# Ranks of kept tokens as sums on TensorE, their comparisons on two engines, and a gate with fewer steps

## The chip, the cores and the metric

One core of one Trainium2 chip. The metric is the device time of one execution in microseconds, as the median of several runs. In the text TensorE is also PE (PEld are its weight loads), VectorE DVE, ScalarE ACT, GpSimd POOL, SyncE SP, as the profile has them.

## The reference

An attention of the delta rule (4 batches, 8 heads, 768 steps, heads of 48) feeds a mixture of experts with a capacity.

```python
for t in range(S):
    y[:, :, t] = einsum('bhd,bhde->bhe', q[:, :, t], state)
    v_old = einsum('bhde,bhd->bhe', state, kt)
    state = state + bt * einsum('bhd,bhe->bhde', kt, vt - v_old)
x = y.transpose(0, 2, 1, 3).reshape(3072, 384)
logits = x @ w_gate                      # 8 experts
expert_idx = argmax(logits, axis=1); gate_w = softmax(logits)[expert_idx]
for e in range(8):                       # at most 80 tokens an expert, the ones with the largest gate_w
    tok_idx = ...
    h = maximum(x[tok_idx] @ w1[e], 0); out[tok_idx] = gate_w[tok_idx] * (h @ w2[e])
```

The rows of tokens that are not kept are zero.

## The kernel before

**The attention loop.** Time is cut in 12 chunks of 64 steps. The loop `for j in range(NC)` (L1038) runs one step of the chain over the chunks and, ahead of it, prepares later chunks: `gram(j + 4)` makes the products of keys, `store` and `fetch` bring their 16x16 diagonal blocks through DRAM, `solve(j + 3)` (L404) inverts these on GpSimd with 14 pairs of small operations between a first product (L410) and a last copy (L418), `result_out` and `spread` bring the inverse back, and the `merge_` functions build the inverse of the whole chunk on TensorE. `scale_k` and `beta_mask` (L333, L338) are GpSimd's too. Chunk by chunk the chain makes R (L527), UB (L539), the new state and the outputs x.

**The order of work.** All of it is written out by hand: each engine executes its instructions in the order in which the program issues them. Work beside the loop is written as generators, which stand in a list `fillers`. `fill(us)` (L258) takes steps from the first one until the costs that they yield add up to `us`; a function that a generator yields waits in `due` until `point()` (L253) runs it. In a step j the calls come in this order: scale_k, beta_mask, chain_ks and `sums(j - 1)` (logits of the last chunk), point, merge_x4, a `fill(2.2)` for 6 <= j < 10, chain_tr, merge_y4, point, `fill(1.5)` (2.8 from j = 6 on), merge_p5, `solve(j + 3)`, chain, loads, outputs and the transposes `both(j + 4)`, `fill(6.6)` (8 from j = 6 on), point, merge_y5, out_t, `gram(j + 4)`, merge_p2, point.

**The gate.** A chunk gives two blocks of 128 tokens, so there are 24 blocks. `gate(m0, nm)` (L603) takes the logits of `nm` blocks and makes a one-hot of the argmax and the weight gw = 1 / sum of exp(logit - max). The exponential is a power of two (`two`, L639, made from the rounded quotient `n`) times a polynomial of the rest r, in Horner steps of one scalar_tensor_tensor each (L611). All of it is on VectorE, a step being 0.25 in the budget of `fill`, but for one call with `g=nc.gpsimd`. It is called for blocks 0 to 7 and 8 to 15 in `sort_group` (L688; appended to the fillers in the `sums` of j = 4 and j = 8), for blocks 16 to 19 on GpSimd at j = 10, and for blocks 20 to 23 after the loop (L1134). `gate_pool` (L673, GpSimd) packs the results for later products.

**The selection.** Blocks 0 to 15 are sorted by max8 operations; `choose_sorted` (L721) keeps at most 80 of them per expert ("old", their weights in AO). The 8 new blocks (16 to 23; `early` are the first four, `late` the others) are then compared with each other and with the old ones, and every token gets its rank:
- `beats` (L863) compares the weights of a group of new blocks, broadcast into GB1 (early) or GB2 (late), with those of block m, one weight per partition. It takes "less" for blocks ahead of m, "less or equal" for blocks behind it, and for m itself a tie mask with the triangle `tri`. The result H (4 buffers) is summed by `count` (L892) on TensorE with the one-hot of block m. For early against early all four calls are on GpSimd, at the end of j = 10 (L1099); the others follow the loop on VectorE.
- `against_old` (L847) compares the broadcast old weights ABC with new blocks (G), VectorE; the sums over G are TensorE's and ScalarE's.
- The rank among the old ones: 16 comparisons of 80x80 on GpSimd (L838, L839), a product with `trl` (L840), a sum (L841), and after the loop a reduction on VectorE (L842) into rankO.

After the loop the program issues: the counts of early against early, the sums over G, the weight loads 0 to 6 (`load_w`, SP queue), the transposes of `bcast_old` and `bcast_new(early)` with copies to ABC and GB1 by ScalarE, the late gate, its gate_pool, GB2, late against early, `against_old(late)`, the reduction into rankO, all against late, then slotO (L1148), one-hots and products that yield the row numbers idx_g.

**The experts.** Eight gathers on GpSimd (L1203) bring the rows; each expert is two groups of 96 pairs of products (L1237), with weights in 10 buffers.

Of the kernel before, what the change touches and what calls it, by code (L numbers as in the profile page):

```python
# [8 lines left out]
F32 = mybir.dt.float32  # L9
# [9 lines left out]
LN2_HI = 0.693145751953125  # L19
LN2_LO = 1.42860682030941723212e-6  # L20
ROUND = 12582912.0


@with_exitstack
def kernel(
# [22 lines left out]
    nc = tc.nc  # L48
# [100 lines left out]
    less = keep.tile([128, NN], F32, name="less")  # L149
    AO = keep.tile([cap, E], F32, name="AO")  # L150
    a5o = keep.tile([cap, E, 5], BF16, name="a5o")
    rankO = keep.tile([cap, E], F32, name="rankO")
    t1 = keep.tile([cap, E, cap], BF16, name="t1")
    tri = const.tile([128, 128], BF16, name="tri")
    nc.gpsimd.memset(tri, 1.0)
    nc.gpsimd.affine_select(out=tri, in_=tri, compare_op=Alu.is_gt, fill=0.0, base=0, pattern=[[1, 128]], channel_multiplier=-1)
    trl = const.tile([128, 128], BF16, name="trl")
    nc.gpsimd.memset(trl, 1.0)
    nc.gpsimd.affine_select(out=trl, in_=trl, compare_op=Alu.is_gt, fill=0.0, base=0, pattern=[[-1, 128]], channel_multiplier=1)
# [26 lines left out]
    with ExitStack() as actx:  # L186
# [71 lines left out]
        def fill(us, flush=False):  # L258

            while us > 0 and fillers:  # L260
                if due:
                    if not flush:
                        return
                    point()
                n = next(fillers[0], None)
                if n is None:
                    fillers.pop(0)
                elif callable(n):
                    due.append(n)
                else:  # L270
                    us -= n
# [331 lines left out]
        def gate(m0, nm, g=nc.vector):  # L603
# [5 lines left out]
            def stt(out, in0, scalar, in1, op0, op1):  # L609
                if g is nc.vector:  # L610
                    g.scalar_tensor_tensor(out=out, in0=in0, scalar=scalar, in1=in1, op0=op0, op1=op1)  # L611
# [27 lines left out]
            g.tensor_scalar(two, n, 127.0, 8388608.0, op0=Alu.add, op1=Alu.mult)  # L639
            yield 0.25  # L640
            r = tile_(full, F32, "r")
            stt(out=r, in0=n, scalar=-LN2_HI, in1=sc, op0=Alu.mult, op1=Alu.add)
            yield 0.25
# [6 lines left out]
            nc.vector.tensor_tensor(out=oh, in0=first, in1=fm.unsqueeze(2).to_broadcast(full), op=Alu.is_equal)  # L650
            yield 0.25
            ex = tile_(full, F32, "ex")
            g.tensor_scalar(ex, r, 1.0 / 5040.0, None, op0=Alu.mult)
            yield 0.25
            for f in (720.0, 120.0, 24.0, 6.0, 2.0, 1.0):
                stt(out=ex, in0=ex, scalar=1.0 / f, in1=r, op0=Alu.add, op1=Alu.mult)
                yield 0.25
            stt(out=ex, in0=ex, scalar=1.0, in1=two.bitcast(F32), op0=Alu.add, op1=Alu.mult)
            yield 0.25
            gw = gwN[:, m0 - NS : m0 - NS + nm] if new else tile_(full[:2], F32, "gw")  # L660
            sm = tile_(full[:2], F32, "sm")
# [11 lines left out]
        def gate_pool(m0, nm):  # L673
            full = [128, nm, E]
            oh, og = ohs[m0]
            rb = rhs[:, m0 : m0 + nm, :, :]
            nc.gpsimd.tensor_tensor(out=rb[:, :, :, 0], op=Alu.mult, in0=oh,
                                    in1=hi[:, m0 : m0 + nm].unsqueeze(2).to_broadcast(full))
            nc.gpsimd.tensor_scalar(rb[:, :, :, 1], oh, pp1[:, 0:1], None, op0=Alu.mult)
            rest = og  # L680
            for j in range(3):
                nc.gpsimd.tensor_copy(rb[:, :, :, 2 + j], rest)
                if j < 2:
                    nxt = gsm.tile([128, NT, E], F32, name=f"rest{j}")[:, :nm]
                    nc.gpsimd.tensor_tensor(out=nxt, in0=rest, in1=rb[:, :, :, 2 + j], op=Alu.subtract)
                    rest = nxt
# [34 lines left out]
        def choose_sorted(sl):  # L721
# [25 lines left out]
            W2 = [sl.tile([E, 2, 128], F32, name=f"W{i}") for i in range(2)]  # L747
# [87 lines left out]
            t2 = sl.tile([cap, E, cap], BF16, name="t2")  # L835
            for e in range(E):
                row, one_ = ABC[:cap, e], AO[:, e : e + 1]
                nc.gpsimd.tensor_scalar(t2[:, e], row, one_, None, op0=Alu.is_equal)  # L838
                nc.gpsimd.tensor_scalar(t1[:, e], row, one_, None, op0=Alu.is_gt)  # L839
            nc.gpsimd.tensor_tensor(out=t2, in0=t2, in1=trl[:cap, :cap].unsqueeze(1).to_broadcast([cap, E, cap]), op=Alu.mult)  # L840
            nc.gpsimd.tensor_tensor(out=t1, in0=t1, in1=t2, op=Alu.add)  # L841
            after.append(lambda: nc.vector.tensor_reduce(rankO, t1, axis=AX, op=Alu.add))  # L842
            yield from against_old(early, ABC, sl)

        counted, after = [], []

        def against_old(ms, ABC, sl):  # L847

# [11 lines left out]
                counted.append(sums_)  # L860
                yield 0.85

        def beats(eng, m, ms, GB, sl, own=True):  # L863

            L = len(ms)
            H = sl.tile([128, NN // 2 * 128], BF16, name="H", bufs=4)[:, : 128 * L]
            g = gwN[:, m : m + 1]
            a = sum(i < m for i in ms) * 128
            b = a + 128 * (m in ms)
            if a:  # L870
                eng.tensor_scalar(H[:, :a], GB[:, :a], g, None, op0=Alu.is_lt)
                yield 0.4
            if b < 128 * L:
                eng.tensor_scalar(H[:, b:], GB[:, b:], g, None, op0=Alu.is_le)
                yield 0.4
            if b > a:
                t = sl.tile([128, 128], BF16, name="tie", bufs=2)
                if eng is nc.vector:
                    eng.scalar_tensor_tensor(out=t, in0=GB[:, a:b], scalar=g, in1=tri, op0=Alu.is_equal, op1=Alu.mult)
                    yield 0.3  # L880
                    eng.scalar_tensor_tensor(out=H[:, a:b], in0=GB[:, a:b], scalar=g, in1=t, op0=Alu.is_lt, op1=Alu.add)
                    yield 0.3
                else:
                    eng.tensor_scalar(t, GB[:, a:b], g, None, op0=Alu.is_equal)
                    eng.tensor_scalar(H[:, a:b], GB[:, a:b], g, None, op0=Alu.is_lt)
                    eng.tensor_tensor(out=t, in0=t, in1=tri, op=Alu.mult)
                    eng.tensor_tensor(out=H[:, a:b], in0=H[:, a:b], in1=t, op=Alu.add)
            Hs[m, ms[0]] = H

        Hs = {}  # L890

        def count(m, ms):  # L892
            H = Hs.pop((m, ms[0]))
            for n, i in enumerate(ms):
                nc.tensor.matmul(S_ps[:, 0, 384 + E * i : 384 + E * i + E], lhsT=H[:, 128 * n : 128 * n + 128], rhs=ohN[:, m, :],
                                 start=False, stop=(m == NN - 1), skip_group_check=True)

        early, late = list(range(NN // 2)), list(range(NN // 2, NN))

# [27 lines left out]
        def drain(steps):  # L927
            for _ in steps:
                pass
# [55 lines left out]
        solve(1)  # L985
        gram(2, send=False)
        heat(16)
        Xbf = blk.tile([128, 512], BF16, name="Xbf")
# [49 lines left out]
        for j in range(NC):  # L1038
# [18 lines left out]
            point()  # L1057
            if j >= NC - 2:
                fill(0.5)
            if j % 2 == 1:  # L1060
                fillers.insert(0, newton(squares([j + 5, j + 6])))
            if j == 0:
# [30 lines left out]
            if j == NC - 2:  # L1093
                fill(1)
                drain(pool_gate)
                point()
                GB1 = s1.tile([128, 128 * len(early)], F32, name="GB1")
                nc.scalar.copy(GB1, bcast_new(early))
                for m in early:  # L1099
                    drain(beats(nc.gpsimd, m, early, GB1, s1))  # L1100
                gate_pool(NS, NN // 2)
            if j == 0:
                for r in rest:
                    r()
# [10 lines left out]
                fill(0.01)  # L1115
            if j == NC - 2:
                fill(5)
        sums(NC - 1)
        for m in early:
            count(m, early)  # L1120
        for f in counted:
# [8 lines left out]
        ab, GB1 = bcast_old(), s2.tile([128, 128 * len(early)], F32, name="GB1")  # L1130
        for h in range(2):
            nc.scalar.copy(ABC[:, 4 * h : 4 * h + 4], ab[:, h, : 4 * cap].rearrange("p (e t) -> p e t", t=cap))
        nc.scalar.copy(GB1, bcast_new(early))
# [8 lines left out]
        for f in counted + after:  # L1142
            f()
        for m in early + late:
            drain(beats(nc.vector, m, late, GB2, s2))
            count(m, late)
        slotO = s2.tile([cap, E], BF16, name="slotO")
        nc.vector.scalar_tensor_tensor(out=slotO, in0=S_ps[:cap, 1, 384 : 384 + E], scalar=1.0, in1=rankO, op0=Alu.add, op1=Alu.add)  # L1148
# [143 lines left out]
```

## Time and profile before

| what | value |
|---|---|
| median of 3 runs | 381.84 us (381.19 to 383.92) |
| profiled execution, own time | 385.28 us |
| its span, first to last instruction | 383.6 us |
| mean granted TensorE clock | 0.931 |
| busy: PE, PEld | 317.6 us (83%), 280.6 us (73%) |
| busy: DVE, ACT, POOL | 210.0 us (55%), 178.0 us (46%), 211.7 us (55%) |
| DMA | 65.29 MB, mean 170 GB/s |

Times in the profile count from the start of the span. In its timeline a row has start, duration, engine, line, operation, tiles (out<-in), shape and count; in square brackets stands how long the engine was idle just before, and what released it. In the rows of 40 slices a digit is the busy share in tenths, and PEclk the granted clock in tenths of full speed. The loop runs to about 267 us, the selection to about 299 us, the experts from there to the end.

### The profile page before, as it was taken

The numbers are of one execution on the slowest core, as the hardware profiler recorded it, in microseconds if no ns is written. First come the engines' busy times: TensorE is split into PE (matmuls) and PEld (weight loads), VectorE is DVE, ScalarE is ACT, GpSimd is POOL, SyncE is SP. The second block draws the span as 40 slices with busy tenths as digits, with TensorE's granted clock in tenths as the row PEclk, the third lists the DMA queues.
The fourth block names the chain that finished last, engine by engine and source line by source line (L and its number), as shares of the span: only waits on it lengthen the run. The fifth ranks groups of instructions, "written<-read, shape, count | busy, mean of one in ns | idle before, by whom it ended". The sixth has DMA issues, their size and how long they took to land. (4 is left out here: it accounts for less than half of the span.)

```text
span 383.6 us, 16917 instructions
## 1 busy us (share of the span) xinstructions
PE 317.6 (83%) x7356; PEld 280.6 (73%) x7356; DVE 210.0 (55%) x533; ACT 178.0 (46%) x362; POOL 211.7 (55%) x513
## 2 busy tenths in 40 slices
PE   8757869899898999798999898978633699796993
PEld 4544568799798988788999788867532399686893
DVE  7958775676247585599435769696649101010110
ACT  3644347576577676474776666553430011111110
POOL 8540786487775757582776384649994611010010
PEclk9998999899999999899999999898555889999999
DMA  9999548887897969665866566351799616999410
GB/s 139 169 165 180 98 65 167 134 169 120 172 143 152 186 104 169 120 128 103 146 109 142 86 181 138 137 192 48 281 392 388 245 43 222 394 396 392 150 26 17
DMA packets 185257, 65.29 MB, mean 170 GB/s; under 512 B 164160, under 2 KB 181568, under 8 KB 185184
## 3 DMA queue, kind: packets, MB, share of 16 engines
q1 hardware_dynamic: 156144, 56.28, 61.6%
q10 hardware_dynamic: 28272, 5.98, 8.2%
q0 software_dynamic: 768, 1.97, 1.7%
q8 instruction: 58, 0.95, 1.0%
q14 instruction: 15, 0.12, 0.1%
HBM read 44.35 MB, written 19.86 MB: 167 GB/s over the span
## 5 line engine op out<-in xcount | busy, mean ns | idle before, releaser
L415 POOL TENSOR_TENSOR tmpTrue<-XY,NT 128x14 f32<-128x14 f32 (+6 forms) x154 | 44.6, 289 | 12.1
L417 POOL TENSOR_TENSOR XY<-XY,tmpTrue 128x14 f32<-128x14 f32 (+6 forms) x154 | 41.8, 272 | 12.1
L1229 POOL DMA_INDIRECT out_dram<-y,idx_s x8 | 7.4, 921 | 63.4 <-DVE y L1228 63.4
L241 PE MATMUL pm<-SB,KQ 128*64 128x96 f32 x704 | 34.4, 249 | 2.0 <-issue 0.8
L410 POOL TENSOR_TENSOR XY<-NT,eye 128x256 f32<-128x256 f32 x11 | 9.4, 853 | 47.6 <-DMA NT<-a_blocks 42.2
L1237 PE MATMUL hp<-xTe,w 128*64 128x80 f32 x768 | 31.7, 241 | 3.9 <-issue 3.4
L539 DVE TENSOR_TENSOR UB<-pm,beta_t 64x768 f32<-64x768 f32 x24 | 22.9, 954 | 20.2 <-PE pm L241 20.0
L1237 PEld LDWEIGHTS hp<-xTe,w 128*64 128x64 f32 x768 | 29.4, 143 | 5.7 <-issue 5.0
L241 PEld LDWEIGHTS pm<-SB,KQ 128*64 128x64 f32 x704 | 30.6, 138 | 4.0 <-PE pm L241 1.9
L381 DVE TENSOR_TENSOR B<-pm,bm 128x512 f32<-128x512 f32 x24 | 16.3, 681 | 28.7 <-PE pm L241 11.6
L1228 DVE TENSOR_SCALAR y<-yp,gw_t 80x384 f32<-80x384 f32 x8 | 4.9, 613 | 49.0 <-PE yp L1226 49.0
L1250 ACT ACTIVATE hT<-hp 128x320 f32<-128x320 f32 x16 | 7.0, 437 | 52.8 <-PE hp L1237 52.8
L1237 PE MATMUL tp<-hT,w 128*64 128x80 f32 x768 | 29.6, 234 | 2.2 <-issue 1.7
L1237 PEld LDWEIGHTS tp<-hT,w 128*64 128x64 f32 x768 | 27.5, 137 | 3.8 <-issue 2.2
L241 PE MATMUL pm<-KQ 48*64 48x128 f32 x768 | 25.8, 287 | 5.0 <-ACT KQ L356 4.9
L241 PEld LDWEIGHTS pm<-KQ 48*64 48x64 f32 x768 | 22.7, 141 | 7.2 <-ACT KQ L356 6.0
L356 ACT COPY KQ<-pm 128x512 f32<-128x512 f32 x48 | 24.8, 611 | 4.8 <-issue 4.2
L467 ACT COPY X<-pm 32x256 f32<-32x256 f32 x44 | 16.0, 364 | 22.4 <-PE pm L241 18.1
L444 ACT ACTIVATE YB<-YD,qm 128x256 f32<-128x256 f32 x48 | 20.5, 499 | 11.6 <-DMA YD<-inv_blocks 11.6
L341 POOL TENSOR_TENSOR bm<-beta_t,neg_strict 128x1024 f32<-128x1024 f32 x12 | 22.8, 1900 | 1.2 <-DVE beta_t L954 1.2
L561 ACT COPY SB<-S_ps 48x768 f32<-48x768 f32 x22 | 17.5, 794 | 11.4 <-PE S_ps L241 11.2
L241 PE MATMUL pm<-R,Y 64*64 64x48 f32 x704 | 15.0, 235 | 5.2 <-issue 4.7
(258 smaller groups left out, 741.6 us busy)
## 6 DMA issues: line engine op xcount, KB each, us to landing
w<-in_moe_w_dram SPq DMA_DIRECT2D x16, 1536.0 KB, 15.9
qn<-in_q_dram SPq DMA_DIRECT2D x24, 192.0 KB, 5.4
a_blocks<-B ACTq DMA_DIRECT2D x18, 256.0 KB, 5.2
vin<-in_v_dram SPq DMA_DIRECT2D x24, 192.0 KB, 4.9
x_rows<-x SPq DMA_DIRECT2D x24, 192.0 KB, 4.0
out_dram<-zero SPq DMA_DIRECT2D x12, 384.0 KB, 4.4
kr<-in_k_dram SPq DMA_DIRECT2D x23, 192.0 KB, 4.9
inv_blocks<-XY SPq DMA_DIRECT2D x11, 256.0 KB, 2.8
```

The lines of the kernel that those rows point to most:

```text
L241: nc.tensor.matmul(out, lhsT=lhsT, rhs=rhs, start=not acc, stop=not acc, skip_group_check=True)
L341: nc.gpsimd.tensor_tensor(out=bms[c], in0=beta_t[:, c].unsqueeze(2).to_broadcast([128, NB, 64]), in1=neg_strict.unsqueeze(1).to_broadcast( ...
L356: nc.scalar.copy(KQs[c][:, 4 * h : 4 * h + 4, n, :], pt[:, h].rearrange("r (g w) -> r g w", w=128))
L381: nc.vector.tensor_tensor(out=own(B1), in0=pv[:, 0], in1=own(bm), op=Alu.mult)
L410: eng.tensor_tensor(out=X, in0=NT.rearrange("p s t -> p t s"), in1=eye16, op=Alu.add)
L415: eng.tensor_tensor(out=tv, in0=X[:, t + 1 :, t : t + 1].to_broadcast(sh), in1=NT[:, 0:t, t].unsqueeze(1).to_broadcast(sh), op=Alu.mult)
L417: eng.tensor_tensor(out=X[:, t + 1 :, 0:t], in0=X[:, t + 1 :, 0:t], in1=tv, op=Alu.add)
L444: nc.scalar.mul(dst, Yd, w)
L467: copy(X4[hs(e, 32), :, h, e], ps[64 * e + 32 * h : 64 * e + 32 * h + 32, 0, :256].rearrange("r (g w) -> r g w", w=32))
L539: nc.vector.tensor_tensor(out=UB[hs(e), :, e].rearrange("r (g c) d -> r c g d", c=2), in0=ps[hs(e), :, : 8 * D].rearrange("r c (g d) -> r ...
L561: nc.scalar.copy(SB[hs(p, D), :, :, p].rearrange("r (b g) e d -> r b (g e) d", b=2), S_ps[hs(p, D), :, : 8 * D].rearrange("r b (g d) -> r ...
L1237: nc.tensor.matmul(out[r], lhsT=lhsT[:, r], rhs=rhs, skip_group_check=True, **kw)
```

## The change

- The gate: `two` is always made on GpSimd, where a further operation makes `scale` from it (a power of two over a constant). The polynomial has other coefficients (EXP) and two steps fewer; its last step multiplies by `scale`. The step of the budget that `two` had is gone.
- `beats` compares with one operation over the whole group, and where block m is in the group it makes a second tile T of ties, from block m to the end of the group, whose first 128 columns are multiplied by `tri`. `count` sums H and T.
- Of early against early, GpSimd keeps blocks 0 and 1; VectorE does block 2 at the beginning of j = 11 and block 3 at its end. The gate_pool of blocks 16 to 19 moves from the end of j = 10 to the end of j = 11.
- The rank among the old ones: the 16 comparisons stay on GpSimd ("less" and "equal" into two tiles `below`), the second is multiplied by `tri`, and TensorE sums both with 16 products of one column each into the sums of `against_old`. The addition, the reduction and rankO are gone.
- The transposes of `bcast_old` and `bcast_new(early)` after the loop stand ahead of the counts, and GB1 is copied ahead of ABC.
- Some tiles share or change their place (W, Xbf, t1, t2, trl).

```diff
+EXP = (722.359314, 722.3593374, 361.1796148, 120.3915103, 30.0992743, 6.049220681)
...
-            g.tensor_scalar(two, n, 127.0, 8388608.0, op0=Alu.add, op1=Alu.mult)
-            yield 0.25
+            nc.gpsimd.tensor_scalar(two, n, 127.0, 8388608.0, op0=Alu.add, op1=Alu.mult)
+            scale = tile_(full, F32, "scale")
+            nc.gpsimd.tensor_scalar(scale, two.bitcast(F32), 1.0 / EXP[0], None, op0=Alu.mult)
...
-            g.tensor_scalar(ex, r, 1.0 / 5040.0, None, op0=Alu.mult)
-            yield 0.25
-            for f in (720.0, 120.0, 24.0, 6.0, 2.0, 1.0):
-                stt(out=ex, in0=ex, scalar=1.0 / f, in1=r, op0=Alu.add, op1=Alu.mult)
+            for n, f in enumerate(EXP[:0:-1]):
+                stt(out=ex, in0=ex if n else r, scalar=f, in1=r, op0=Alu.add, op1=Alu.mult)
                 yield 0.25
-            stt(out=ex, in0=ex, scalar=1.0, in1=two.bitcast(F32), op0=Alu.add, op1=Alu.mult)
+            stt(out=ex, in0=ex, scalar=EXP[0], in1=scale, op0=Alu.add, op1=Alu.mult)
...
-                nc.gpsimd.tensor_scalar(t2[:, e], row, one_, None, op0=Alu.is_equal)
-                nc.gpsimd.tensor_scalar(t1[:, e], row, one_, None, op0=Alu.is_gt)
-            nc.gpsimd.tensor_tensor(out=t2, in0=t2, in1=trl[:cap, :cap].unsqueeze(1).to_broadcast([cap, E, cap]), op=Alu.mult)
-            nc.gpsimd.tensor_tensor(out=t1, in0=t1, in1=t2, op=Alu.add)
-            after.append(lambda: nc.vector.tensor_reduce(rankO, t1, axis=AX, op=Alu.add))
+                nc.gpsimd.tensor_scalar(below[0][:, e], row, one_, None, op0=Alu.is_lt)
+                nc.gpsimd.tensor_scalar(below[1][:, e], row, one_, None, op0=Alu.is_equal)
+            nc.gpsimd.tensor_tensor(out=below[1], in0=below[1], in1=tri[:cap, :cap].unsqueeze(1).to_broadcast([cap, E, cap]), op=Alu.mult)
...
+            eng.tensor_scalar(H, GB, g, None, op0=Alu.is_le if m < ms[0] else Alu.is_lt)
+            yield 0.46
+            T = None
+            if m in ms:
+                a = 128 * ms.index(m)
+                T = sl.tile([128, 128 * L - a], BF16, name=f"T{a}")
+                eng.tensor_scalar(T, GB[:, a:], g, None, op0=Alu.is_equal)
                 yield 0.4
+                eng.tensor_tensor(out=T[:, :128], in0=T[:, :128], in1=tri, op=Alu.mult)
+                yield 0.25
+            Hs[m, ms[0]] = H, T
...
+            if j == NC - 1:
+                drain(beats(nc.vector, early[2], early, GB1, s1))
             if j % 2 == 1:
                 fillers.insert(0, newton(squares([j + 5, j + 6])))
...
-                for m in early:
+                for m in early[:2]:
                     drain(beats(nc.gpsimd, m, early, GB1, s1))
-                gate_pool(NS, NN // 2)
...
+            if j == NC - 1:
+                drain(beats(nc.vector, early[3], early, GB1, s1))
+                gate_pool(NS, NN // 2)
         sums(NC - 1)
+        wide = bcast_old(), bcast_new(early)
         for m in early:
             count(m, early)
...
+        for t in below:
+            for x in range(E):
+                nc.tensor.matmul(S_ps[:cap, 1, 384 + x : 385 + x], lhsT=t[:, x, :], rhs=ones_b[:cap, 0:1], start=False, stop=False,
+                                 skip_group_check=True)
         for m in early + late:
             drain(beats(nc.vector, m, late, GB2, s2))
             count(m, late)
...
-        nc.vector.scalar_tensor_tensor(out=slotO, in0=S_ps[:cap, 1, 384 : 384 + E], scalar=1.0, in1=rankO, op0=Alu.add, op1=Alu.add)
+        nc.vector.tensor_scalar_add(slotO, S_ps[:cap, 1, 384 : 384 + E], 1.0)
```

More of the change, by code (lines that the diff above doesn't have):

```diff
@@ L151 @@
     a5o = keep.tile([cap, E, 5], BF16, name="a5o")
-    rankO = keep.tile([cap, E], F32, name="rankO")
-    t1 = keep.tile([cap, E, cap], BF16, name="t1")
+    below = [keep.tile([cap, E, cap], BF16, name=f"below{i}") for i in range(2)]
     tri = const.tile([128, 128], BF16, name="tri")
@@ L156 @@
     nc.gpsimd.affine_select(out=tri, in_=tri, compare_op=Alu.is_gt, fill=0.0, base=0, pattern=[[1, 128]], channel_multiplier=-1)
-    trl = const.tile([128, 128], BF16, name="trl")
-    nc.gpsimd.memset(trl, 1.0)
-    nc.gpsimd.affine_select(out=trl, in_=trl, compare_op=Alu.is_gt, fill=0.0, base=0, pattern=[[-1, 128]], channel_multiplier=1)
     ioti = const.tile([128, cap], I32, name="ioti")
@@ L746, in choose_sorted @@
             yield rows
-            W2 = [sl.tile([E, 2, 128], F32, name=f"W{i}") for i in range(2)]
+            W2 = [sl.tile([E, 2, 128], F32, name="W"), mg[:, :2]]
             for n in range(2):
@@ L834, in choose_sorted @@
             yield wide
-            t2 = sl.tile([cap, E, cap], BF16, name="t2")
             for e in range(E):
                 row, one_ = ABC[:cap, e], AO[:, e : e + 1]
-                nc.gpsimd.tensor_scalar(t2[:, e], row, one_, None, op0=Alu.is_equal)
-                nc.gpsimd.tensor_scalar(t1[:, e], row, one_, None, op0=Alu.is_gt)
-            nc.gpsimd.tensor_tensor(out=t2, in0=t2, in1=trl[:cap, :cap].unsqueeze(1).to_broadcast([cap, E, cap]), op=Alu.mult)
-            nc.gpsimd.tensor_tensor(out=t1, in0=t1, in1=t2, op=Alu.add)
-            after.append(lambda: nc.vector.tensor_reduce(rankO, t1, axis=AX, op=Alu.add))
+                nc.gpsimd.tensor_scalar(below[0][:, e], row, one_, None, op0=Alu.is_lt)
+                nc.gpsimd.tensor_scalar(below[1][:, e], row, one_, None, op0=Alu.is_equal)
+            nc.gpsimd.tensor_tensor(out=below[1], in0=below[1], in1=tri[:cap, :cap].unsqueeze(1).to_broadcast([cap, E, cap]), op=Alu.mult)
             yield from against_old(early, ABC, sl)
-        counted, after = [], []
+        counted = []
         def against_old(ms, ABC, sl):
@@ L861, in against_old, with beats @@
                 yield 0.85
-        def beats(eng, m, ms, GB, sl, own=True):
-            L = len(ms)
+        def beats(eng, m, ms, GB, sl):
+            L, g = len(ms), gwN[:, m : m + 1]
             H = sl.tile([128, NN // 2 * 128], BF16, name="H", bufs=4)[:, : 128 * L]
[L867 to L871, printed above, removed]
-                yield 0.4
[L873 to L888, printed above, removed]
@@ L890 @@
         Hs = {}
         def count(m, ms):
-            H = Hs.pop((m, ms[0]))
+            H, T = Hs.pop((m, ms[0]))
             for n, i in enumerate(ms):
-                nc.tensor.matmul(S_ps[:, 0, 384 + E * i : 384 + E * i + E], lhsT=H[:, 128 * n : 128 * n + 128], rhs=ohN[:, m, :],
-                                 start=False, stop=(m == NN - 1), skip_group_check=True)
+                for left in (H[:, 128 * n : 128 * n + 128], T[:, 128 * (i - m) : 128 * (i - m) + 128] if T is not None and i >= m else None):
+                    if left is not None:
+                        nc.tensor.matmul(S_ps[:, 0, 384 + E * i : 384 + E * i + E], lhsT=left, rhs=ohN[:, m, :],
+                                         start=False, stop=(m == NN - 1), skip_group_check=True)
@@ L987 @@
         heat(16)
-        Xbf = blk.tile([128, 512], BF16, name="Xbf")
+        Xbf = vec.tile([128, 512], BF16, name="Xbf", tag="x")
         xy0 = Xss[0]
@@ L1129 @@
         ABC = s2.tile([128, E, cap], F32, name="ABC")
-        ab, GB1 = bcast_old(), s2.tile([128, 128 * len(early)], F32, name="GB1")
+        GB1 = s2.tile([128, 128 * len(early)], F32, name="GB1")
+        nc.scalar.copy(GB1, wide[1])
         for h in range(2):
-            nc.scalar.copy(ABC[:, 4 * h : 4 * h + 4], ab[:, h, : 4 * cap].rearrange("p (e t) -> p e t", t=cap))
-        nc.scalar.copy(GB1, bcast_new(early))
+            nc.scalar.copy(ABC[:, 4 * h : 4 * h + 4], wide[0][:, h, : 4 * cap].rearrange("p (e t) -> p e t", t=cap))
         drain(gate(NS + NN // 2, NN // 2))
@@ L1141 @@
         drain(against_old(late, ABC, s2))
-        for f in counted + after:
+        for f in counted:
             f()
+        for t in below:
+            for x in range(E):
+                nc.tensor.matmul(S_ps[:cap, 1, 384 + x : 385 + x], lhsT=t[:, x, :], rhs=ones_b[:cap, 0:1], start=False, stop=False,
+                                 skip_group_check=True)
         for m in early + late:
```

## Prediction

> **What bounds the kernel now.** I read the page first. Its slices show TensorE (PE) nearly full until about 240 us, then a dip, then a last stage in which it is nearly full again; the granted clock is at half speed in the dip.
>
> ```profile
> PE   8757869899898999798999898978633699796993
> PEclk9998999899999999899999999898555889999999
> ```
>
> A slice is 9.59 us. So there are two regimes: up to slice 27 what holds up TensorE costs time one for one; in slices 28 to 30 (269 to 298 us) a serial selection on VectorE (DVE) and GpSimd (POOL) does. Then I read the timeline of the selection, engine by engine:
>
> ```profile
> 262.82 3.46 DVE L851 TENSOR_TENSOR G<-ABC,ohg 128x640 bf16<-128x640 f32 x4
> 268.80 1.29 POOL L871 TENSOR_SCALAR H<-GB,gwN 128x384 bf16<-128x384 f32 x1
> 272.99 0.19 DVE L611 SCALAR_TENSOR_TENSOR ex<-ex,two 128x32 f32<-128x32 f32 x1
> 274.24 0.50 POOL L838 TENSOR_SCALAR t<-ABC,AO 80x80 bf16<-80x80 f32 x1
> 277.27 1.86 DVE L871 TENSOR_SCALAR H<-GB,gwN 128x512 bf16<-128x512 f32 x4 [3.15 <-ACT GB L1133]
> 279.05 3.07 DVE L851 TENSOR_TENSOR G<-ABC,ohg 128x640 bf16<-128x640 f32 x4
> 286.13 1.39 POOL L841 TENSOR_TENSOR t<-t,t 80x640 bf16<-80x640 bf16 x1
> 287.55 0.81 DVE L842 TENSOR_REDUCE rankO<-t 80x8 f32<-80x640 bf16 x1 [5.43 <-POOL t L841]
> 294.44 0.16 DVE L1148 SCALAR_TENSOR_TENSOR slotO<-S_ps,rankO 80x8 bf16<-80x8 f32 x1 [0.28 <-PE S_ps L895]
> ```
>
> VectorE is in order, and its two idle spells set the stage's end: 3.15 us for the broadcast GB1, behind the counts on TensorE (which wait for GpSimd's H), and 5.43 us for GpSimd's rank among kept tokens. Third, the loop where the gate of the first 8 blocks runs (j = 4):
>
> ```profile
> 139.96 0.20 DVE L639 TENSOR_SCALAR two<-n 128x64 int32<-128x64 f32 x1
> 142.09 0.85 POOL L410 TENSOR_TENSOR XY<-NT,eye 128x256 f32<-128x256 f32 x1 [4.50 <-DMA NT<-a_blocks]
> 143.35 0.26 DVE L611 SCALAR_TENSOR_TENSOR ex<-ex,two 128x64 f32<-128x64 f32 x1
> 144.35 0.24 DVE L669 TENSOR_TENSOR ohg<-oh,gw 128x64 f32<-128x64 bf16 x1
> 144.74 0.38 PE L695 MATMUL pm<-ident,ohg 128*32 128x128 f32 x2 [1.21 <-DVE ohg L669]
> 152.90 0.62 POOL L418 COPY XY<-XY 128x256 f32<-128x256 f32 x1
> ```
>
> Here the gate is on VectorE alone, while GpSimd sits in inverse 7 from 142.09 (and before that waits for its data) to 153.5. TensorE's transposes of the gate's result already wait 1.21 us for VectorE.
>
> **What the Trainium skill says.** "Trainium Architecture — The Big Picture" (Inside one NeuronCore): each engine has its own instruction stream, and they meet only at semaphores; so work handed to GpSimd starts when GpSimd's stream reaches it. The trace agrees: GpSimd's rank operations come at 274.24, behind its comparisons, though their input ABC was there at 262.8. "SBUF — State Buffer" (SBUF: two separate sides): VectorE and GpSimd share a port pair under an exclusive lock. The trace agrees in direction: a 128x128 comparison on GpSimd takes 0.60 us, and 1.66 us (at 256.58) beside VectorE's two G products. "TensorE: Matmul & The Clock Gate" (Part 1): an idle TensorE falls to half clock after about 3.4 us. Here a 2.14 us hole at 154 was followed by a clock of 0.62 (156 to 159) and 0.81 (159 to 162).
>
> **The change part by part.** Sums are against the profiled execution: span 383.6 us, own time 385.28; the runs' median is 381.84, that is 3.4 below it, and I carry the difference over to it.
>
> *Gate, first 8 blocks: the exponent moves to GpSimd.* `two` and a new `scale` are always on GpSimd. Which step issues them? At j = 4 `fill(1.5)` takes six steps of 0.25, up to the second `n`; the trace shows just six gate instructions ahead of the merge copy at 139.23. The seventh step now issues `two` and `scale`, in `fill(6.6)`, which stands after `solve(7)`. So on GpSimd they queue behind scale_k(8), beta_mask(8), the 4.5 us wait for NT, and inverse 7, whose last copy ends at 152.90 + 0.62 = 153.5. Price of the two 128x64 operations: the trace has 128x32 ones at 0.22 to 0.29 and a bf16 128x64 at 0.57, so 0.45 to 1.15 for both; I take 0.8: `scale` is there at 154.3. VectorE's last polynomial step waits for it from 142.6 (143.35 less the three removed steps, some 0.7). From this step to the end of `ohg` is 144.59 - 143.35 = 1.24 us, and a semaphore 0.1 to 0.2: TensorE's transposes start at about 155.75 instead of 144.74. **+11.0 us.** What is queued behind: on VectorE the copies and masks of gram(8), merge 6 and R of step 5; on TensorE everything (merge_y5, out_t, gram(8), the next step), since it is in order and these transposes stand first. TensorE is busy 0.95 of the time from here to 262 and its idle spells there are its own waits on VectorE and ScalarE, which move with it; a lead of DMA and GpSimd therefore buys little. Two corrections: after 12 us of idleness the clock is cold for some 4 us (the restart at 156.1 cost 1.72 for 1.15, 1.92 for 1.09, 1.64 for 1.54: 1.5 us), and the present hole at 154 (2.14, put down to "issue", with its own 1.5 of cold clock) may vanish or not: -3.6 to 0. I take +1.5 - 1.5 = 0, ends +1.5 and -2.1.
>
> *Gate, next 8 blocks (j = 8).* `fill(2.2)` allows nine steps before solve(11), so `two` and `scale` go ahead of it; GpSimd is idle from 209.7 to 216.3. 0 us; three short VectorE steps fewer, hidden under TensorE.
>
> *GpSimd gate of blocks 16 to 19.* A step less and one more: it ended at 249.6, its successor waits until 255.15 for GB. 0.
>
> *Comparisons of early blocks.* GpSimd keeps two of four. From 128x384 at 1.29, 128x256 at 0.93, 128x128 at 0.60 a 128x512 is 1.63. m0: 1.63 + 1.63 + 0.43; m1: 1.63 + 1.29 + 0.43; 7.0 us clean. Locked times: about 1.2 under VectorE's two G, 0.9 under its new comparison of m2, 2.2 under the four G at 262.82. 255.15 + 11.3 = 266.4, before it was 272.2. On VectorE m2 costs 0.46 + 0.37 + 0.2 = 1.0 us, under the 1.54 us in which it waits for UB's product; m3 about 1.0 in the 2.09 us before `lg`. 0 us; without that cover up to 1.0 each.
>
> *Rank among kept tokens.* GpSimd: 16 comparisons at 0.475 (7.6), one product 1.38; the second product (1.39) and VectorE's reduction go. From 266.4, 0.5 lost under m3: ends at 275.9. Then gate_pool(NS), now behind it, 2.1: 278.0. Then the *late gate's* `two` and `scale`, 0.6: 278.6. VectorE, which now reaches its last polynomial step at about 272, waits till then. From there 272.99 to 274.12 is 1.13: gate done at 279.8. Before, VectorE resumed at 277.27; GB1 is now early (transposes ahead of the counts, copies by about 272), so its 3.15 us wait is replaced by this one: **+2.5**. After it: 1.86 + 3.07 to 284.75, GB2 long there, and the 5.43 us wait and the 0.81 us reduction are gone: **-6.2**.
>
> *Late comparisons.* Before 5.86 us (288.29 to 294.15). Now eight of 0.40, ties of 512, 384, 256, 128 (0.40 + 0.37 + 0.34 + 0.29) and four products of 0.2: 5.4. TensorE has 16 more sums of 0.07 in front (the 32 of L857 took 2.27) and 10 tie products; with four H buffers VectorE may wait 0.5, and the last tie products stand 0.2 ahead of slotO: 6.1. **+0.3**. slotO comes at about 291.0 in the old time frame against 294.44: -3.4. GpSimd's last gate_pool (2.1 us, before 287.48 to 292.5) now starts at 279.9 and is done by then.
>
> *Hand over to the experts.* Weights 0 to 6 are loaded from 271.72 to about 301.5 without pause, whatever the selection does; the first gather now starts 3.4 us earlier, inside that traffic. A gather took 5.3 us to land at most (the first), 3.1 in the median:
>
> ```profile
> 299.27 1.20 POOL L1203 DMA_INDIRECT xg<-x_rows,idx_g  x1 [6.76 <-DVE gw_t L1189]
> 304.89 0.40 PE L1212 MATMUL xp<-ident,xg 80*128 80x80 f32 x3 [3.15 <-issue]
> ```
>
> Ends 0 and +3; scatters under full traffic landed in 6.2 at most, a microsecond above: **+0.7**. The rest (Xbf, W and tri tiles in other places) issues nothing new: 0.
>
> Sum: 11.0 + 0 - 3.4 + 0.7 = **+8.3**: span 391.9, own time 393.6, and 390.1 on the median. I put down 390.0.
>
> **Rivals.**
> 1. *Likeliest, 0.64: as summed.* Own range 386.5 to 393.5 (-2.1 or +1.5 for hole and clock, 1.5 either way for GpSimd's locked times, up to 0.4 more for the gathers).
> 2. *The stall is partly repaid, 0.14.* The hole at 154 goes with its cold clock (-3.6) and GpSimd is 2 us earlier in the selection: +8.3 - 2.1 - 2 = +4.2 or less: 384 to 386. For it: GpSimd is idle 4.5 us in that step. Against: its input then is DMA from gram 7, not slack.
> 3. *The gate doesn't wait, faster, 0.09.* If `two` and `scale` run ahead of inverse 7, only the selection is left: -3.4 + 0.7: 379.1; if the late pair is ahead of the rank as well, VectorE resumes at about 273.3 in place of 279.8, 6.5 less: 372.6. Decides: `scale` of the first gate before 142.6. Against it: the program order in `fill`, and that GpSimd's order in the trace follows the code.
> 4. *The selection gives nothing, 0.13.* GpSimd starves under VectorE's comparisons (at 287.70 a 0.42 us operation took 3.06), `scale` comes at 282 and the gathers wait for the weights: +11 + 1.5: 394. For it: the lock; against: VectorE stands still while `scale` is awaited.
>
> **How the numbers follow.** About 1% (3.8 us) is what a measurement tells from no change here. Slower: nearly all of 1 and 4 and a third of 2, 0.80. Same: two thirds of 2, edges of 1: 0.11. Faster: 0.09. The range, 384.5 to 394.0, holds 1, most of 2 and half of 4.
>
> **What would show it.** Right: VectorE's first gate has an idle spell of about 11 us put down to GpSimd's `scale`, and L695's transposes wait as long; UB of step 5 moves from 156.5 to about 167; in the selection VectorE waits 6 to 7 us for the second `scale` and not at all for the rank; slotO comes at about 302 (294.4 + 11.0 - 3.4). Wrong: `scale` seen ahead of inverse 7, or TensorE's transposes at their old place in the step.

## The result and the profile after

| | before | after |
|---|---|---|
| median on the same chip | 382.51 us (381.19 to 383.92, 4 runs) | 399.06 us (397.71 to 401.76, 4 runs) |
| ratio | | 1.0441 [1.0372, 1.051] |
| profiled execution, own time and span | 385.28, 383.6 us | 401.76, 400.0 us |
| mean granted TensorE clock | 0.931 | 0.913 |

Slower, as predicted, but by 16.6 us instead of 8.3, and outside the range. The profiled execution of after is the slowest of its four.

The slices of the page after (10 us each) show two dips of TensorE where the page before has one: the new one is in slice 16, and the granted clock falls there too.

```profile
PE   8748869879998950698799989898836689797994
PEclk9996999999999995699899999989855669999999
```

**The first gate (j = 4).** Rows of the timeline of after: start, duration, engine, line, operation, tiles; in brackets the idle time just before, and what ended it.

```profile
147.20 0.84 POOL L408 TENSOR_TENSOR XY<-NT,eye 128x256 f32<-128x256 f32 x1 [5.35 <-DMA NT<-a_blocks]
157.94 0.60 POOL L416 COPY XY<-XY 128x256 f32<-128x256 f32 x1
158.95 0.38 POOL L639 TENSOR_SCALAR scale<-two 128x64 f32<-128x64 f32 x1
159.30 1.46 POOL L333 TENSOR_TENSOR kn<-kr,inv 128x768 f32<-128x768 f32 x1
159.36 1.49 DVE L609 SCALAR_TENSOR_TENSOR ex<-ex,scale 128x64 f32<-128x64 f32 x1 [14.07 <-POOL scale L639]
160.74 1.89 POOL L339 TENSOR_TENSOR bm<-beta_t,neg_strict 128x1024 f32<-128x1024 f32 x1
161.14 1.51 DVE L661 TENSOR_SCALAR sm<-sm 128x8 f32<-128x8 f32 x1
163.30 0.59 PE L692 MATMUL pm<-ident,ohg 128*32 128x128 f32 x2 [16.13 <-DVE ohg L666]
```

The first three rows are the order that the prediction gave: inverse 7, its last copy, then `scale`. VectorE stands 14.07 us for it, TensorE 16.13 us for VectorE. Two rows were not foreseen: VectorE's last polynomial step takes 1.49 us (0.26 before), and the addition of a constant to 8 columns (`sm`) takes 1.51 us (0.17 before). Each ends within 0.1 us of the GpSimd operation beside it.

**The selection.** The same view, later:

```profile
293.34 1.39 POOL L836 TENSOR_TENSOR below<-below,tri 80x640 bf16<-80x640 bf16 x1
297.23 0.29 POOL L639 TENSOR_SCALAR scale<-two 128x32 f32<-128x32 f32 x1
297.55 0.22 DVE L609 SCALAR_TENSOR_TENSOR ex<-ex,scale 128x32 f32<-128x32 f32 x1 [5.49 <-POOL scale L639]
300.17 3.08 DVE L845 TENSOR_TENSOR G<-ABC,ohg 128x640 bf16<-128x640 f32 x4
309.40 0.16 DVE L1143 TENSOR_SCALAR slotO<-S_ps 80x8 bf16<-80x8 f32 x1 [0.28 <-PE S_ps L881]
```

The waits of 3.15 us (for GB1) and 5.43 us (for the rank) are gone; one of 5.49 us for the second `scale` stands in their place. The last UB (chunk 11) starts at 280.78 here and at 260.79 before, so slotO, 20.0 us earlier, would be at 289.4 in the old frame: 5.0 us ahead of 294.44.

**The hand-over.** First gather and first product that uses it:

```profile
314.25 1.19 POOL L1198 DMA_INDIRECT xg<-x_rows,idx_g  x1 [13.08 <-DMA w<-in_moe_w_dram]
320.82 0.63 PE L1207 MATMUL xp<-ident,xg 80*128 80x80 f32 x3 [3.18 <-issue]
```

6.57 us lie between them, 5.62 before; gathers land in 6.2 us in the median, 3.1 before. The 5.62 was a slow one. In the six profiles of kernels with the old selection this stretch takes 3.7 to 5.6 us, 4.4 in the mean; in the nine with the new one it takes 6.2 to 6.6 us, 6.4 in the mean.

**Stages.** I cut the span at the starts of UB in the timeline (UB4 is chunk 4's) and at slotO. One profiled execution each, us; the last two columns speak of the DMA queue that carries all plain loads and stores (busy time is its share times the span) and of kr's median time from issue to landing. The kernels are those of the next section. The rows come from several chips: on that of b_pad32, b_pad_in, b_pad_rest and a_best the kernel before itself took 390.4 us (median), so their stages are not to be set against the first row. In this document a ratio leaves out slow executions, those over 1.5% above the fastest of their kernel, and the profiles of a_gate_vector and a_pad32_again are of such executions.

| kernel | start to UB4 | UB4 to UB5 | UB5 to UB11 | UB11 to slotO | slotO to end | queue busy | kr lands |
|---|---|---|---|---|---|---|---|
| before | 134.8 | 21.7 | 104.3 | 33.7 | 89.2 | 236.3 | 4.8 |
| after | 137.0 | 37.2 | 106.6 | 28.6 | 90.6 | 253.2 | 5.5 |
| a_gate_vector | 140.1 | 21.8 | 105.8 | 24.8 | 91.0 | 252.7 | 5.5 |
| a_earlier_step | 139.8 | 21.2 | 105.4 | 28.5 | 89.8 | 248.6 | 5.5 |
| b_first_two_pool | 136.6 | 34.0 | 103.9 | 34.5 | 85.2 | 236.1 | 5.0 |
| a_pad32 | 134.9 | 33.2 | 103.5 | 28.2 | 89.7 | 237.3 | 4.9 |
| a_same | 137.3 | 33.7 | 103.9 | 28.6 | 91.0 | 250.8 | 5.5 |
| a_pad32_again | 137.6 | 33.8 | 105.1 | 28.5 | 91.1 | 240.0 | 4.9 |
| a_pad64 | 136.9 | 34.3 | 105.5 | 28.6 | 90.3 | 244.9 | 5.4 |
| b_pad32 | 135.3 | 21.9 | 105.9 | 34.4 | 92.4 | 244.5 | 5.4 |
| b_pad_in | 139.6 | 21.7 | 106.7 | 34.5 | 93.8 | 247.2 | 5.8 |
| b_pad_rest | 135.1 | 21.2 | 106.7 | 34.5 | 93.6 | 240.1 | 4.9 |
| a_best | 139.9 | 19.8 | 104.8 | 25.0 | 91.3 | 240.3 | 4.9 |
| b_all | 133.9 | 21.5 | 104.7 | 34.4 | 85.3 | 235.8 | 5.0 |
| a_best_all | 134.2 | 22.5 | 106.2 | 23.9 | 90.8 | 237.2 | 5.1 |

The two stages of the change, UB4 to UB5 and UB11 to slotO, come out within a few us of the prediction: in after, a_same, a_pad64 and a_pad32 the first grows by 11.5 to 15.4 us (11.0 predicted) and the second shrinks by 5.0 to 5.4 (3.4 predicted). What doesn't is the rest: after loses 2.2 us ahead of UB4, where the change adds no operation, 2.3 between UB5 and UB11, and its loads keep the queue busy 17 us longer with the same packets and bytes. (a_same, the same kernel, loses 2.5 ahead of UB4 too, but nothing between UB5 and UB11.) That pointed to the step that I had priced at nothing: tiles in other places.

### The profile page after: what moved, and what is told of

The parts are those of the page before. It is cut to its first block, busy times and chain, and to the rows that moved or that the text cites. A ratio compares the mean times of both kernels' runs of the same rounds, so it can differ in the third digit from the quotient of the medians.

```text
span 400.0 us, 16968 instructions
## 1 busy us (share of the span) xinstructions
PE 320.6 (80%) x7390; PEld 283.6 (71%) x7392; DVE 210.4 (53%) x527; ACT 177.9 (44%) x362; POOL 199.8 (50%) x498
## 5 line engine op out<-in xcount | busy, mean ns | idle before, releaser
L413 POOL TENSOR_TENSOR tmpTrue<-XY,NT 128x14 f32<-128x14 f32 (+6 forms) x154 | 43.8, 284 | 12.1
L239 PE MATMUL pm<-SB,KQ 128*64 128x96 f32 x704 | 35.3, 253 | 3.6 <-issue 1.8
L1232 PE MATMUL hp<-xTe,w 128*64 128x80 f32 x768 | 32.9, 245 | 3.7 <-issue 3.2
L239 PEld LDWEIGHTS pm<-SB,KQ 128*64 128x64 f32 x704 | 31.5, 141 | 5.7 <-issue 3.9
L1232 PEld LDWEIGHTS hp<-xTe,w 128*64 128x64 f32 x768 | 30.5, 146 | 5.7 <-issue 4.9
L379 DVE TENSOR_TENSOR B<-pm,bm 128x512 f32<-128x512 f32 x24 | 16.3, 681 | 33.7 <-PE pm L239 33.6
L239 PE MATMUL pm<-X,B 128*32 128x64 f32 x384 | 14.3, 227 | 8.5 <-issue 4.7
```

Of the source, the lines that this page charges most:

```text
L239: nc.tensor.matmul(out, lhsT=lhsT, rhs=rhs, start=not acc, stop=not acc, skip_group_check=True)
L379: nc.vector.tensor_tensor(out=own(B1), in0=pv[:, 0], in1=own(bm), op=Alu.mult)
L413: eng.tensor_tensor(out=tv, in0=X[:, t + 1 :, t : t + 1].to_broadcast(sh), in1=NT[:, 0:t, t].unsqueeze(1).to_broadcast(sh), op=Alu.mult)
L1232: nc.tensor.matmul(out[r], lhsT=lhsT[:, r], rhs=rhs, skip_group_check=True, **kw)
```

## The experiments

Each ratio is to the kernel before on the same chip, with its 95% interval. Names that begin with a_ start from the kernel after, with b_ from the kernel before.

**1. The gate on VectorE again (a_gate_vector).** `g` is VectorE for the three gates that VectorE runs.

```diff
-            nc.gpsimd.tensor_scalar(two, n, 127.0, ...)
+            g.tensor_scalar(two, n, 127.0, ...)
...
-            nc.gpsimd.tensor_scalar(scale, two.bitcast(F32), ...)
+            g.tensor_scalar(scale, two.bitcast(F32), ...)
```

> The changed kernel with `two` and `scale` on VectorE again for the gates that are on VectorE; all else as changed. Theory (GpSimd's queue makes both gates wait): the step from UB of chunk 4 to UB of chunk 5 loses its extra 15.4 us, and VectorE's wait of 5.5 us for the late `scale` goes: 399.1 - 15.4 - 5.5 = 378. Rival (the loss is from the moved tiles or the other edits): 390 or more.

Measured: 0.9896 [0.9858, 0.9934].

```profile
148.16 0.32 DVE L609 SCALAR_TENSOR_TENSOR ex<-ex,scale 128x64 f32<-128x64 f32 x1
150.36 0.38 PE L692 MATMUL pm<-ident,ohg 128*32 128x128 f32 x2
```

No bracket in either row: both waits are gone, and UB4 to UB5 is 21.8 us again. UB11 to slotO is 24.8 us, 3.8 less than in after and 8.9 less than before. So the selection's gain is real, and the gate's place on GpSimd costs more than all of it.

**2. Only the place in GpSimd's queue (a_earlier_step).** The two operations stay on GpSimd; one more step at j = 4 lets them go ahead of `solve(7)`.

```diff
-                fill(1.5 if j < 6 else 2.8)
+                fill((1.75 if j == 4 else 1.5) if j < 6 else 2.8)
```

> The changed kernel, but the fill of 1.5 at j = 4 is 1.75, so that `two` and `scale` of the first gate are issued just ahead of inverse 7; they stay on GpSimd. Theory (place in GpSimd's queue): the first stall of 14 us goes, the late wait of 5.5 us stays: 399.1 - 15.4 = 383.7. Rival (the hand-over to GpSimd costs by itself): 397 to 399.

Measured: 1.0043 [0.9999, 1.0087]. In the view of VectorE's waits (total us, times, longest) only the late one is left:

```profile
DVE ex L609 <- POOL scale L639: 6.5, 1, 6.5
```

What costs is the queue, not GpSimd's speed: one number in a budget takes back some 4% (after itself had 1.0441 and 1.0417, on other chips). The late wait is the difference to experiment 1: 1.5%, some 5.6 us, against the 5.49 and 6.5 us of the two profiles.

**3. The first wait, in the kernel before (b_first_two_pool).** `two` of blocks 0 to 7 goes to GpSimd, nothing else; no tile moves.

```diff
-            g.tensor_scalar(two, n, 127.0, 8388608.0, ...)
+            g2 = nc.gpsimd if m0 == 0 else g
+            g2.tensor_scalar(two, n, 127.0, 8388608.0, ...)
```

> The kernel before with one edit: `two` of blocks 0 to 7 is made on GpSimd (no `scale`, no tile moved). Theory: VectorE waits for inverse 7 and TensorE with it, 13 to 16 us: 396 to 398. Rival (part of the loss between UB of chunks 4 and 5 comes from tiles that stand 32 bytes off): 11, as predicted: 393.5.

Measured: 1.0212 [1.0127, 1.0297].

```profile
154.74 0.60 POOL L418 COPY XY<-XY 128x256 f32<-128x256 f32 x1
155.43 0.24 POOL L640 TENSOR_SCALAR two<-n 128x64 int32<-128x64 f32 x1
155.71 0.23 DVE L611 SCALAR_TENSOR_TENSOR ex<-ex,two 128x64 f32<-128x64 f32 x1 [10.82 <-POOL two L640]
155.75 1.51 POOL L335 TENSOR_TENSOR kn<-kr,inv 128x768 f32<-128x768 f32 x1
156.22 1.07 DVE L665 TENSOR_SCALAR sm<-sm 128x8 f32<-128x8 f32 x1
157.23 1.90 POOL L341 TENSOR_TENSOR bm<-beta_t,neg_strict 128x1024 f32<-128x1024 f32 x1
157.56 1.64 DVE L670 TENSOR_TENSOR ohg<-oh,gw 128x64 f32<-128x64 bf16 x1
159.35 0.58 PE L696 MATMUL pm<-ident,ohg 128*32 128x128 f32 x2 [13.95 <-DVE ohg L670]
```

One operation of 0.24 us in another engine's queue costs 12.2 us in its step (34.0 against 21.7). Not all of it is the wait: the two VectorE operations beside kn and bm take 1.07 and 1.64 us (0.17 and 0.24 before), which is 2.3 us. And over the whole kernel the ratio gives less, 8.1 us (4.9 to 11.4): the two profiles also differ by -4.0 us behind slotO, where the edit has no part. One profile against one is the rougher measure, so the edit costs some 8 to 12 us.

**4. The tiles moved back (a_pad32).** Tiles are laid out one behind the other. Worked out from the built programs, in bytes of a partition: the change takes away trl (256), rankO (32) and t1 (1280) and adds two `below` (1280 each) and two `scale` (256 each). So kr moves from 36,224 to 37,728, vin from 45,440 to 46,944; the weights start where kr does; the tiles of q, XB, B1 and x and nearly all others of the loop move with them. All these were at multiples of 64 and are 32 off after; NT, XY and YD changed the other way. The 32 bytes of rankO make the odd half. An unused tile of 32 bytes turns it back and issues nothing.

```diff
+    pad32 = keep.tile([128, 8], F32, name="pad32")
     below = [keep.tile(
```

> The changed kernel with an unused tile of 32 bytes ahead of `below`, so that the loaded tiles (k, q, v), the outputs x and B1 start at a multiple of 64 bytes again, as before the change; NT, YD and XY then don't, as before. Theory (the 2.2 us lost ahead of j = 4 and the 3.2 us at j = 6 are slower transfers): 399.1 - 3 to 5.5 = 394 to 396. Rival (they are the scatter of single runs): 399.

Measured: 1.0219 [1.0139, 1.0298], against 1.0441 for after (on another chip, hence experiment 5).

```profile
140.13 0.90 POOL L409 TENSOR_TENSOR XY<-NT,eye 128x256 f32<-128x256 f32 x1 [4.83 <-DMA NT<-a_blocks]
151.94 0.38 POOL L640 TENSOR_SCALAR scale<-two 128x64 f32<-128x64 f32 x1
152.36 1.49 DVE L610 SCALAR_TENSOR_TENSOR ex<-ex,scale 128x64 f32<-128x64 f32 x1 [9.34 <-POOL scale L640]
```

The waits of the gate are still there; without the offset the change costs 2.2%, some 8.4 us (5.3 to 11.4 by the interval), and the predicted sum was 8.3.

**5. After again, and a control of the size (a_same, a_pad64, a_pad32_again).** a_same is the kernel after without an edit. a_pad64 has 64 unused bytes in the place of the 32, which moves all tiles behind it but leaves every remainder to 64 as after has it; a_pad32_again repeats experiment 4 beside it.

```diff
+    pad64 = keep.tile([128, 16], F32, name="pad64")
     below = [keep.tile(
```

> The changed kernel as it is, on one chip with b_all and a_best_all, and for a ratio with more runs. If the three costs add up (first gate's wait 11 to 12, tiles 32 bytes off 3 to 8, selection -3 to -5): 1.025 to 1.045 of before; first result 1.044, with the 32 bytes 1.022.

Measured: 1.0417 [1.0359, 1.0475].

> Control for a_pad32: the changed kernel with an unused tile of 64 bytes at the same place, so that every later tile moves, but k, q, v, XB, x and B1 stay 32 bytes off a multiple of 64. Theory (the remainder by 64 decides): as the changed kernel, 1.042 of before. Rival (any move of the addresses, or scatter): as a_pad32, 1.022.

Measured: 1.037 [1.032, 1.042].

> a_pad32 once more, on the same chip as a_pad64: the same tile of 32 bytes. Theory: 1.022 of before, 0.980 of a_pad64. Rival: the two are equal.

Measured: 1.0245 [1.0191, 1.0298], on the chip of a_pad64. Not the move counts, but the remainder: 64 bytes leave the time at 1.037, 32 take 1.25% off it (4.8 us). From the two intervals I estimate 0.5 to 2.0% for this difference.

**6. The offset in the kernel before (b_pad32, b_pad_in, b_pad_rest, b_all).** b_pad32 has 32 bytes ahead of rankO. b_pad_in has a second 32 bytes ahead of `kn`, so that only kr, vin and the weights are off. b_pad_rest has the second alone: q, XB, B1 and x are off (and NT, XY and YD on multiples of 64). b_all puts 32 bytes in the pool of small tiles, so that NT, XY and YD are on multiples of 64 as well.

```diff
+    pad32 = keep.tile([128, 8], F32, name="pad32")        # b_pad32, b_pad_in
     rankO = keep.tile(
...
+        pad32b = blk.tile([128, 8], F32, name="pad32b")   # b_pad_in, b_pad_rest
         kn = [blk.tile(
...
         warm = sml.tile([128, 1], F32, name="warm", bufs=1)
+        pad32w = sml.tile([128, 8], F32, name="pad32w", bufs=1)   # b_all
```

> The kernel before with an unused tile of 32 bytes ahead of rankO and nothing else, which puts k, q, v, XB, x, B1 and the weights 32 bytes off a multiple of 64, and NT, YD, XY on one: the state of the changed kernel. Theory (the tiles' place costs as much in the old kernel as in the new one, where 32 bytes took 399 to 391): slower by 1.5 to 2.2%. Rival (it costs only where the gate waits for NT): within 0.5%.

Measured: 1.008 [1.0046, 1.0113].

> The kernel before with two unused tiles of 32 bytes, ahead of rankO and ahead of kn: only kr, vin and the weights stand 32 bytes off a multiple of 64, the other tiles as before. Theory A (the loads of k and v are what gets slower): most of the loss of b_pad32. Theory B (q, XB, B1 and x are): 0.

Measured: 1.0121 [1.0048, 1.0194].

> The kernel before with one unused tile of 32 bytes ahead of kn: kr, vin and the weights as before, q, XB, B1 and x 32 bytes off, and NT, YD, XY on a multiple of 64. Theory A (loads of k and v): 0 or a little faster. Theory B (q, XB, B1, x): most of the loss of b_pad32.

Measured: 1.0034 [0.9999, 1.0068].

> The kernel before with one unused tile of 32 bytes ahead of ss, so that NT, XY and YD too start at a multiple of 64 bytes; k, q, v, B1 and x do already. Theory (each transfer between DRAM and a tile gains from it): NT and YD land 0.3 to 0.4 us sooner, 0 to 0.5% faster, as GpSimd waits for NT but TensorE doesn't wait for GpSimd. Rival (only the loads of 192-byte rows gain): no difference.

Measured: 0.9956 [0.9926, 0.9986].

32 unused bytes make the kernel before slower by about 0.8%, and kr, vin and the weights are enough for it (1.2% in b_pad_in). Of q, XB, B1 and x the interval reaches no effect, but b_pad_rest also has the offset of b_all, which alone took 0.4% off; so a cost of some 0.8% can hide there. The cause of b_all's 0.4% is not shown. Four pages side by side, the queue's packets, MB and share, and the loads of kr with KB each and the median to landing. Before:

```profile
q1 hardware_dynamic: 156144, 56.28, 61.6%
...
kr<-in_k_dram SPq DMA_DIRECT2D x23, 192.0 KB, 4.9
```

b_pad32:

```profile
q1 hardware_dynamic: 156144, 56.28, 62.7%
...
kr<-in_k_dram SPq DMA_DIRECT2D x23, 192.0 KB, 5.4
```

After:

```profile
q1 hardware_dynamic: 156144, 56.28, 63.3%
...
kr<-in_k_dram SPq DMA_DIRECT2D x23, 192.0 KB, 5.5
```

a_pad32:

```profile
q1 hardware_dynamic: 156144, 56.28, 60.9%
...
kr<-in_k_dram SPq DMA_DIRECT2D x23, 192.0 KB, 5.0
```

The packets and bytes are the same in all four; with the tiles 32 off, the share times the span is 244.5 and 253.2 us in place of 236.3 and 237.3, and kr lands half a microsecond later, in both kernels. (A page counts the 23 loads of kr that the queue issues, the table all 24, hence 4.9 and 4.8 for before.)

The packets of the traces tell more. On this queue only the rows of k, q and v are 192 bytes, and the weights come in packets of 1536 (with some stores among these) and 4096. Busy time over the 16 engines, us:

| packets | 8 profiles with kr, vin and weights on multiples of 64 | 7 profiles with them 32 off |
|---|---|---|
| 192 bytes, 72,704 of them | 86.0 to 89.6 | 92.1 to 101.2 |
| 1536 bytes, 14,336 of them | 64.3 to 65.7 | 65.2 to 66.6 |
| 4096 bytes, 3,072 of them | 31.8 to 33.1 | 32.0 to 32.9 |

So nearly all of the longer queue time is in the small rows, and the weights have little or no part in it. b_pad_rest, where q's tiles are off and kr, vin and the weights are not, stays at 89.2 us, and its q lands in 5.1 us (5.4 before): no loss shows there. The engines that read the tiles are no slower: GpSimd's kn from kr takes 1473 ns in the median before and 1474 in b_pad_in, VectorE's R from vin 548 in both.

**7. Both repaired (a_best, a_best_all).** a_best is experiments 1 and 4 together; a_best_all has b_all's 32 bytes too.

> The changed kernel with `two` and `scale` on VectorE for VectorE's gates and the unused tile of 32 bytes of a_pad32. If both costs are separate, 0.990 of before less 2.0%: 0.970, some 371. If the 32 bytes only matter where the gate waits for NT: 0.990.

Measured: 0.9721 [0.965, 0.9791].

> a_best with the same further 32 bytes ahead of ss, so that NT, XY and YD are on a multiple of 64 as well. a_best was 0.972 of before. Theory: 0.968 to 0.972. Rival (only the loads gain): 0.972.

Measured: 0.9801 [0.9736, 0.9865], on another chip; the intervals overlap, so the last 32 bytes are worth nothing that shows. Both are faster than before: with the gate on VectorE and the tiles moved back the change gains 2 to 3%.

## Why the prediction was right in direction and half in size

- **First gate, +11.0 us: right.** The stage grows by 12.2 us in the kernel before (experiment 3, 8.1 by the ratio) and by 11.5 in a_pad32. One term was missing, +2.6 us here and +2.3 in experiment 3. When `scale` comes, GpSimd goes straight on to kn and bm, and two of VectorE's next operations end only with those: 1.49 us for 0.26, 1.51 for 0.17. The Trainium skill, "SBUF — State Buffer" (Who interferes with whom), has it: a VectorE instruction with two SBUF inputs contends with a GpSimd instruction that reads SBUF, and whoever comes first keeps the shared ports until its end. The trace agrees for the polynomial step, which has two inputs. The addition has one; the same section counts tensor_scalar among the operations that can contend, and the trace shows 1.51 us for it beside bm. I had used that lock on GpSimd's operations alone. In a_pad32 it doesn't show in the sum, since inverse 7 started 5.25 us after UB4 instead of 7.34: 11.0 + 2.6 - 2.1 = 11.5, measured 11.5. In the profile of after inverse 7 started 10.22 us after UB4: 11.0 + 2.6 + 2.9 = 16.5, measured 15.4. a_same has 6.4 us and a_pad64 6.0, so these 2.9 us are that execution's, not the kernel's.
- **Clock and hole, 0: not refuted.** The hole of 2.14 us at 154 is gone from the profile of after, and so is the clock of 0.50 that followed it before (156.8 to 160.0). In its place the restart is cold: the granted clock is 0.53 from 163.3 to 167.0, and L692's products take 0.59 us for 0.38. The 1.1 us between 16.5 and 15.4 is all that I can assign to both.
- **Gates at j = 8 and j = 10, early comparisons, 0: right.** UB5 to UB11 is 103.5 us in a_pad32 and 104.3 before, with a scatter of some 3 us over the table.
- **Selection, -3.4 us: right in its waits, too small.** It is -5.0 in after and -5.4 in a_pad32. In the old frame the second `scale` ended at 277.5 instead of 278.6, and from there slotO took 11.9 us instead of 12.4.
- **Hand-over, +0.7 us: right in its kind, probably too small.** From the first gather to its first use it is +1.0 against the profile before, and +2.1 between the means of the nine profiles and the six (6.4 and 4.4). The whole stage slotO to end doesn't tell it: in kernels with the old selection it lies between 85.2 and 93.8 us.
- **The sum of these, +8.3 us: partly luck.** Without the offset it was measured at some 8.4 and 9.4 us (1.0219 and 1.0245). The missing 2.6 us of the gate and the short hand-over stand against a selection that gained 1.6 to 2 us more.
- **The step that failed:** "The rest (Xbf, W and tri tiles in other places) issues nothing new: 0." It issues nothing new, but the tiles that are loaded behind the removed 32 bytes start at another remainder to 64. This costs the kernel after 1.25% on one chip (1.037 and 1.0245), 4.8 us of the excess of 8.3 (16.6 less 8.3). By a_pad32 against the runs of after on other chips it is 2.0 to 2.2%, about 8 us, which would be all of it; with the gate on VectorE, a_best against a_gate_vector, also on two chips, it is 1.8%. So the term is 5 to 8 us instead of 0, and up to 3.5 us of the excess are not shown on one chip. Where in the span it falls, single profiles don't settle: UB4 starts at 138.0 us in the mean of seven profiles with kr, vin and weights 32 off (135.3 to 140.1) and at 135.9 in the mean of the eight others (133.9 to 139.9).
- **Rival 3** put the time at 372.6 us, 0.976 of before, if neither gate waited. That is what a_best and a_best_all come to: 0.9721 and 0.9801. Its condition failed in the kernel after, as the prediction argued, but its sum was good.

**Open.** That the remainder costs time is shown in both kernels, and that the rows of k and v are slower and land later; why the hardware takes longer is not, nor by which waits the later loads lengthen the span. The Trainium skill, "DMA: Bandwidth & Descriptors" (How a descriptor splits into AXI transactions), says that a descriptor that doesn't start on a multiple of 256 bytes pays for bytes below its start. That is a cause of the right kind. But the page says it of what is read, and here the tile is written. Of kr's rows, 192 bytes one behind the other, one in four starts on such a multiple from 36,224 and none from 37,728, so three in four are off in both kernels; no run here separates this cause from others. kr and vin were not moved one by one. Nor is it settled whether the offset costs the kernel after more than the kernel before: 1.25 to 2.2% against 0.8% (b_pad32), or 1.2% with an interval that reaches 1.9% (b_pad_in).

## What to carry to other kernels

When an operation goes to another engine, look up what stands ahead of it in that engine's program at the step where it is issued, not how busy the engine is: here 0.24 us of work cost some 8 to 12 us behind an inverse, and one more step in a budget took it back. A tile that is added, removed or resized moves all tiles behind it: compare the addresses modulo 64 of what DMAs fill with small rows, and if a profile shows the same packets and bytes at a longer queue time, try an unused pad before looking for a new wait. When a change gives with one hand and takes with the other, undo its parts one by one; here the parts that helped were worth 2 to 3% alone.

## What the runs showed of the hardware

- 32 bytes of an unused tile ahead of kr and vin changed the time of a kernel by 0.8 to 2.2%; 64 bytes by nothing that shows (a_pad64 1.037, a_same 1.0417 on another chip).
- Loads in rows of 192 bytes kept the queue busy 92.1 to 101.2 us where the tiles of k and v start 32 off a multiple of 64, and 86.0 to 89.6 us where they don't; packets of 1536 and 4096 bytes took nearly the same time in both.
- A busy GpSimd holds up VectorE, and not only the other way round: adding a constant to 8 columns lasted 1.51 us on VectorE beside GpSimd's mask of 1.89 us, and 0.17 us where GpSimd was inside its small operations (before, at 143.91).
- Gathers issued into the full stream of weights land in 6.2 us (median; 4.9 to 6.7); the same ones 3.1 us at its end.
